# Attention and gated feed-forward on one core: casts of two batches at a projection, transposes in the gate/value parts, whole-tile stores, part of an exchange on Pool

## The chip, the cores and the metric

The kernel runs on one core of a Trainium2 chip. The metric is the device time of one execution in microseconds (us). Engines are named as the profile names them: PE (TensorE), DVE (VectorE), ACT (ScalarE), POOL (GpSimd) and SP (SyncE, which here only issues DMAs).

## What is computed

Attention without softmax, eight batches of twelve heads, 448 positions, 64 wide; then a gated feed-forward layer over all 3584 rows. Inputs and output are fp32; the kernel works in bf16 with fp32 accumulation.

```
scores = scale * q @ k.T                   # per batch and head, 448 x 448
attn   = max(scores, 0)**2 / S
x      = (attn @ v)  -> rows (batch, position), columns (head, d): 3584 x 768
out    = (max(x @ w_gate, 0) * (x @ w_val)) @ w_out      # 768 -> 1536 -> 768
```

## The kernel before

**Stages.** `first_batch` computes the attention of batch 0. Then for b = 1 to 7 the kernel runs the gate/value product of batch b-1 (`gv_units`, twelve units of 128 columns of d_ff, twelve steps of four matmuls each) with the attention of batch b woven in. `evenly` and `spread` do this: a list of events (score tiles, value passes, loads) is put between steps (unit, step) of the gate/value product. After the even b = 2, 4 and 6 and at the end, `out_pair` projects a pair of batches with w_out. Each engine's and queue's order is the order of the program (`pin`).

**Scores.** `tile_of` computes one pair of score tiles into one of two double PSUM banks; ACT takes the relu into `r_sb` (L230, four buffers), DVE squares it into `attn` (L231, two buffers of one quad each). There are 21 such tiles in a batch, in three quads (`qd`) of four heads. `values` multiplies a quad by v; ACT and DVE copy the result into `x[0]`, and `exchange` copies it with its halves of 64 partitions swapped into `x[1]` (L259). The gate/value product of the next stage reads both.

**Keys and queries.** `T_b` (`kqT`) holds them transposed, in two buffers used by even and odd batches. Batches 0 and 1 are transposed on PE (`transposes`). For the others, `load_qk(b)` casts keys and queries to bf16 in DRAM (two DMAs of POOL, `ks` and `qs`), and `dma_transposes(b, t)` transposes them into `kqT` by DMAs of SP: seven for the keys (L186), one for the queries (L179). `hold(b)` (L522) is a pair of tiny POOL copies out of `kqT`; since POOL works in order, the loads behind it are issued after the transposes have landed.

**When.** Before the change: casts of 2 after the first batch; its transposes in the last two units of b = 1, then a hold, w_out and casts of 3; transposes of 3 in the first projection; a hold, casts of 4 and v at b = 3; and so on, each cast behind a hold on the transposes before it. The transposes of 6 are issued in the second projection.

**The projection.** `out_pair` computes two blocks each way with seven block products instead of eight (A are the blocks of the hidden values `hT`, B of w_out). DVE forms sums of A blocks first (`sums`, L367). Sums of B blocks are formed once, by `weight_sums(0)` to `weight_sums(3)` (L324), in the last four units of b = 2: the third makes T2 and the fourth T4, both in `o_ring`. PE's products follow in the order A11·B11, A12·B21, A11·T2, S1·T1, A21·B12, A22·T4, A12·B22, each over four row tiles (three of 128 rows, one of 64). `keep` (ACT, L359) takes a product out of PSUM and `add` (DVE, L363) adds another. The results lie in the two `attn` buffers until `store_rows` (L377) has stored them; each tile's two halves of 64 rows go out by two DMAs, one of POOL and one of SP.

Of the kernel before, what the change touches and what calls it, by code (L numbers as in the profile page):

```python
# [16 lines left out]
def kernel(  # L17
# [22 lines left out]
    nc = tc.nc  # L40
# [28 lines left out]
    def pin(ins):  # L69
        return tc.keep_in_program_order(ins)  # L70
# [184 lines left out]

    def exchange(b, qd):
        a = slice(2 * qd, 2 * qd + 2)
        for (_, p), (_, other) in zip(HALVES, HALVES[::-1]):
            pin(nc.vector.tensor_copy(x_of[b][1][p, a, :], x_of[b][0][other, a, :]))  # L259

    def values(b, qd, ps):
        value_passes(b, qd, ps, 0, NC)
# [63 lines left out]
    def out_pair(b0, last, aside=None):  # L326
# [41 lines left out]

        def store_rows(t, r, c0, c1, engines):
            s0, n = tiles[t]  # L370
            for c in range(2):
                src = o_sb[2 * t + r][c * 64:c * 64 + 64, c0:c1, :]
# [4 lines left out]
                pin(engines[c].dma_start(out=rows[:, c0:c1, :], in_=src))  # L377

        pool, sync = ((e, e) for e in (nc.gpsimd, nc.sync))
        both, ends = (nc.gpsimd, nc.sync), (nc.sync, nc.scalar)  # L380
        for group in (((0, 1), (2, 3)) if last else ((0, 1, 2, 3),)):
            early = last and group[-1] == 3
            cols = slice(tiles[group[0]][0], sum(tiles[group[-1]]))
            sums(S1, A21, A22, ALU.add, cols)
            sums(A21, A11, A21, ALU.subtract, cols)
            for t in group:
                product(P, t, A11, B11, True)
                keep(t, 0, 0)
            sums(A11, S1, A11, ALU.subtract, cols)
# [36 lines left out]
    STRAIGHT = [(e, hp) for e in range(2) for hp in range(HP)]  # L426

# [121 lines left out]
    def turned(b, u0, u1):  # L549

        return [(u, 1, lambda t=t: dma_transposes(b, t)) for t, u in enumerate((u0, u1))]

    def held(b, u, *some):

        return [(u, 2, lambda: [hold(b)] + [load(c) for load, c in some if c < B])]

    new_x(0)
    units = gv_units(0)
# [3 lines left out]
    for b in range(1, B):  # L562
# [4 lines left out]
        events = evenly(units, {1: 2, 2: 4}.get(b, 0), last, events_of(b)) + [(last, 5, values_event(b, 2))]  # L567
# [46 lines left out]
```

## Time and profile before

| | |
|---|---|
| runs of the kernel | 418.74, 421.94, 415.93 us (median 418.74) |
| the profiled execution | 418.96 us, span 416.9 us, mean granted PE clock 0.997 |
| chain that ended last | PE 84%, DVE 6%, ACT 4%, issue 3%, DMA 3% |
| DMA | 44.26 MB in 155367 packets; POOL's queues 69.3% of 16 engines' span, SP's 20.4% |
| gate/value matmuls (L73, ps<-x,gv) | 4608 of 64x448, 253.2 us busy |
| relus of the scores (L230) | 168, mean 929 ns |
| squares (L231) | 168, mean 623 ns |
| exchange copies (L259) | 48, mean 444 ns |
| sums of A blocks (L367, 128x1344) | mean 850 ns, started some 770 ns apart |
| weight sums (L324) | 4, mean about 1350 ns |
| key and query transposes | 42 DMAs (median issue 1.25 us) and 6 (3.4 us) |

The span runs from the first to the last instruction; the execution's time is 2.06 us longer. The shares in the chain are of the work that ended last, followed back from the end. A line of a timeline holds the start, the time taken, the engine, the line of the kernel, the operation, its output and inputs and how many are merged; in brackets, the engine's idle time before it and what ended that. "SPq" and "ACTq" are DMA issues. In the view by stretches the columns are the stretch, its length, busy time (and instructions) of PE, PEld, DVE, ACT and POOL, PE's granted clock, DMA share and GB/s.

### The profile page before, as it was taken

How to read it: one execution, taken by the hardware profiler on the slowest of the kernel's cores; microseconds unless marked ns; L12 is line 12 of the kernel's file. 1: busy time of each engine (PE TensorE's matmuls, PEld its weight loads, DVE VectorE, ACT ScalarE, POOL GpSimd, SP SyncE). 2: the span in 40 equal slices, each digit the busy share in tenths (PEclk: the TensorE clock that was granted, in tenths of full speed). 3: DMA queues.
4: the chain of work that ended last, by engine and by line, in shares of the span. 5: the costliest groups of instructions: out<-in, count | busy, mean ns of one | idle time of the engine just before them, and what ended most of it. 6: DMA issues, size and time to landing. Idle time of an engine off the chain costs nothing.

```text
span 416.9 us, 16663 instructions
## 1 busy us (share of the span) xinstructions
PE 399.2 (96%) x7536; PEld 275.7 (66%) x7536; DVE 254.9 (61%) x449; ACT 235.4 (56%) x353; POOL 92.0 (22%) x123
## 2 busy tenths in 40 slices
PE   7899997999999998999999999999999999999994
PEld 4466775776776655776677677777777666666673
DVE  4986883589924775866743576676762567422551
ACT  4963991697335775767513877677623777322221
POOL 8834500630007303204304700020002100000040
PEclk9999999999999999999999999999999999999998
DMA  9999999799918995998998992460003600000053
GB/s 157 183 195 195 183 130 119 128 187 138 139 35 252 125 135 94 107 90 110 126 104 201 210 123 32 94 90 4 2 3 83 185 3 3 3 2 4 2 177 91
DMA packets 155367, 44.26 MB, mean 106 GB/s; under 512 B 131136, under 2 KB 153024, under 8 KB 155296
## 3 DMA queue, kind: packets, MB, share of 16 engines
q0 software_dynamic: 117376, 28.67, 69.3%
q1 hardware_dynamic: 37328, 14.03, 20.4%
q8 instruction: 59, 0.97, 1.0%
q10 hardware_dynamic: 592, 0.49, 0.5%
q14 instruction: 12, 0.10, 0.1%
HBM read 47.19 MB, written 19.27 MB: 159 GB/s over the span
## 4 chain that ended last, share of the span: by engine, by line
PE 84%; DVE 6%; ACT 4%; issue 3%; DMA 3%; SPq 0%; DVEq 0%; ACTq 0%
PE ps L73 82%; ACT r_sb L230 3%; DVE attn L231 3%; DMA out_dram<-attn 2%; DMA kr<-in_k_dram 1%; PE ps L206 1%; DVE kqT L207 1%; DVE hT L297 0%; DVE attn L363 0%; PE ps L215 0%; DVE qn L324 0%; DVE x L490 0%; SPq L377 0%; DVE x L259 0%; DVE kn L127 0%
## 5 line engine op out<-in xcount | busy, mean ns | idle before, releaser
L73 PE MATMUL ps<-x,gv 64*64 64x448 bf16 x4608 | 253.2, 349 | 4.2 <-issue 3.4
L73 PEld LDWEIGHTS <-gv 64*64 64x64 bf16 x4608 | 155.1, 107 | 72.8 <-issue 8.3
L230 ACT ACTIVATE r_sb<-ps 128x896 bf16<-128x896 f32 x168 | 149.1, 929 | 28.3 <-PE ps L73 24.2
L231 DVE TENSOR_TENSOR attn<-r_sb 128x896 bf16<-128x896 bf16 x168 | 102.8, 623 | 53.8 <-ACT r_sb L230 44.2
L297 DVE TENSOR_TENSOR hT<-ps,g_sb 128x448 bf16<-128x448 f32 x96 | 59.4, 620 | 34.1 <-ACT g_sb L296 33.6
L296 ACT ACTIVATE g_sb<-ps 128x448 bf16<-128x448 f32 x96 | 52.3, 546 | 48.2 <-PE ps L73 48.1
L73 PEld LDWEIGHTS <-hT 128*64 128x64 bf16 x1152 | 61.2, 110 | 22.6 <-issue 1.7
L73 PE MATMUL ps<-kqT 64*64 64x448 bf16 x672 | 69.2, 351 | 3.0 <-ACT r_sb L230 2.8
L359 ACT ACTIVATE attn<-ps 128x384 f32<-128x384 f32 x64 | 28.8, 450 | 61.1 <-PE ps L73 60.6
L73 PE MATMUL ps<-wo,hT 128*64 128x384 bf16 (+1 forms) x768 | 57.7, 306 | 0.0
L377 POOL DMA_DIRECT2D out_dram<-attn x32 | 17.6, 551 | 178.2 <-ACT attn L359 171.0
L363 DVE TENSOR_TENSOR attn<-ps,attn 128x384 f32<-128x384 f32 (+1 forms) x48 | 22.7, 503 | 45.0 <-ACT attn L359 27.7
L73 PE MATMUL ps<-attn,vn 64*64 64x448 bf16 x672 | 38.4, 350 | 2.6 <-issue 2.1
L73 PEld LDWEIGHTS <-kqT 64*64 64x64 bf16 x672 | 27.3, 106 | 16.5 <-issue 6.5
L73 PEld LDWEIGHTS <-vn 64*64 64x64 bf16 x672 | 23.6, 107 | 12.7 <-issue 4.4
L73 PE MATMUL ps<-o_ring,hT 128*64 128x384 bf16 (+1 forms) x384 | 29.6, 306 | 0.1
L263 ACT ACTIVATE x<-ps 128x448 bf16<-128x448 f32 x21 | 11.4, 543 | 30.3 <-PE ps L73 30.3
L115 POOL DMA_DIRECT2D vn<-in_v_dram x36 | 23.7, 677 | 13.3 <-DVE hT L297 5.0
L522 POOL COPY flag<-kqT 128x1 bf16<-128x1 bf16 x12 | 2.6, 231 | 107.1 <-DMA kqT<-ks 91.1
L259 DVE COPY x<-x 64x896 bf16<-64x896 bf16 x48 | 21.3, 444 | 2.7
L264 DVE CAST x<-ps 128x448 bf16<-128x448 f32 x21 | 13.1, 623 | 15.0 <-PE ps L73 14.9
L115 POOL DMA_DIRECT2D qs<-in_q_dram x6 | 14.8, 2462 | 4.3 <-issue 4.3
(43 smaller groups left out, 134.2 us busy)
## 6 DMA issues: line engine op xcount, KB each, us to landing
out_dram<-attn SPq DMA_DIRECT2D x22, 192.0 KB, 4.1
out_dram<-attn POOLq DMA_DIRECT2D x22, 192.0 KB, 4.4
ks<-in_k_dram POOLq DMA_DIRECT2D x6, 672.0 KB, 13.3
qs<-in_q_dram POOLq DMA_DIRECT2D x6, 672.0 KB, 17.1
vn<-in_v_dram POOLq DMA_DIRECT2D x14, 192.0 KB, 13.5
gv<-in_moe_w_gate_dram POOLq DMA_DIRECT2D x6, 384.0 KB, 11.7
gv<-in_moe_w_val_dram POOLq DMA_DIRECT2D x6, 384.0 KB, 11.4
wo<-in_moe_w_out_dram POOLq DMA_DIRECT2D x2, 1152.0 KB, 11.7
```

The costliest lines, as they stand in the source:

```text
L73: pin(nc.tensor.matmul(o, lhsT=l, rhs=r, start=start, stop=stop, skip_group_check=True))
L115: pin(nc.gpsimd.dma_start(out=o, in_=i))
L230: pin(nc.scalar.activation(r, src, AF.Relu))
L231: pin(nc.vector.tensor_tensor(dst, r, r, ALU.mult))
L259: pin(nc.vector.tensor_copy(x_of[b][1][p, a, :], x_of[b][0][other, a, :]))
L263: pin(nc.scalar.activation(x_of[b][0][:, 2 * qd, :], ps[:, 0, :S], AF.Copy))
L264: pin(nc.vector.tensor_copy(x_of[b][0][:, 2 * qd + 1, :], ps[:, 1, :S]))
L296: pin(nc.scalar.activation(g_sb, o[0], AF.Relu, scale=float(out_scale)))
L297: pin(nc.vector.tensor_tensor(hT[:, mf, col:col + S], o[1], g_sb, ALU.mult))
L359: pin(nc.scalar.activation(out_of(t, r, c), bank(P, t), AF.Copy))
L363: pin(nc.vector.tensor_tensor(o, bank(Q, t), o, ALU.add))
L377: pin(engines[c].dma_start(out=rows[:, c0:c1, :], in_=src))
```

## The change

- `exchange`: for b > 0 and the first two of three quads, POOL makes the two copies instead of DVE.
- Casts: `load_v(b + 2)`, `load_qk(b + 2)` and `load_qk(b + 3)` are issued just ahead of the projection after an even b. All holds but that on batch 2 are gone.
- Transposes: both parts of a batch are issued in one place (`turned`): unit 2 of a stage for b + 1, and for batch 3 the unit before the last of b = 2. For b = 1 the call stands in that branch (unit before the last) and also in the branch that all b but 2 pass through (unit 2).
- b = 1: its PE transposes and score tiles are spread from earlier steps.
- Weight sums: the first two in the last two units of b = 2, the other two in the first projection, behind the sums of A12.
- Stores: `out_pair(0)` keeps two DMAs for a tile; later pairs store a tile of 128 rows by one. Odd results (r = 1) go out by ACT, even ones by SP, none by POOL but in the last group.

```diff
     def exchange(b, qd):
         a = slice(2 * qd, 2 * qd + 2)
+        engine = nc.gpsimd if b > 0 and qd < NQ - 1 else nc.vector
         for (_, p), (_, other) in zip(HALVES, HALVES[::-1]):
-            pin(nc.vector.tensor_copy(x_of[b][1][p, a, :], x_of[b][0][other, a, :]))
+            pin(engine.tensor_copy(x_of[b][1][p, a, :], x_of[b][0][other, a, :]))
...
         def store_rows(t, r, c0, c1, engines):
             s0, n = tiles[t]
+            src = o_sb[2 * t + r]
+            if n == WHOLE and b0 >= NB:
+                row = (b0 + r) * S + s0
+                rows = out[row:row + n, :].rearrange("j (h m) -> j h m", h=2)
+                pin(engines[0].dma_start(out=rows[:, c0:c1, :], in_=src[:, c0:c1, :]))
+                return
             for c in range(2):
...
-        pool, sync = ((e, e) for e in (nc.gpsimd, nc.sync))
-        both, ends = (nc.gpsimd, nc.sync), (nc.sync, nc.scalar)
+        pool, sync, act = ((e, e) for e in (nc.gpsimd, nc.sync, nc.scalar))
+        ends = ((nc.sync, nc.scalar), (nc.scalar, nc.sync))
...
             sums(A12, A12, A11, ALU.subtract, cols)
-            if aside:
-                aside()
+            if first:
+                weight_sums(2)
+                weight_sums(3)
             for t in group:
                 product(P, t, A11, T2, False)
...
                     if not early:
-                        store_rows(t, 1, 0, 2, both)
+                        store_rows(t, 1, 0, 2, act)
                 if early:
                     for t in ts:
-                        store_rows(t, 1, 0, 1, ends)
+                        store_rows(t, 1, 0, 1, ends[0])
...
                     if early:
-                        store_rows(t, 0, 1, 2, ends)
+                        store_rows(t, 0, 1, 2, ends[1])
                     else:
-                        store_rows(t, 0, 0, 2, both)
+                        store_rows(t, 0, 0, 2, sync)
...
+    def turned(b):
+        for t in range(2):
+            dma_transposes(b, t)
+
+    def loads(*some):
+        return lambda: [load(b) for load, b in some if b < B]
...
         if b == 1:
-            events += [(1, 2 + 4 * qd, transposes_event(1, qd)) for qd in range(NQ)]
-            events += turned(2, last - 1, last) + [(last, 2, lambda: (hold(2), load_wo(), load_qk(3)))]
-        elif b == 2:
-            events += [(1, 1, lambda: load_v(3))]
-            events += [(8 + n, 3, lambda n=n: weight_sums(n)) for n in range(4)]
-        elif b == 3:
-            events += held(3, 0, (load_qk, 4), (load_v, 4)) + turned(4, 5, 6) + held(4, 7, (load_qk, 5))
-        elif even:
-            events += turned(b + 1, 1, 2) + held(b + 1, 3, (load_v, b + 1), (load_qk, b + 2)) if b + 1 < B else []
+            events = evenly(units, 1, last, [None] * 2 + events_of(b))[2:]
+            events += [(n, 8 - 4 * (n == 1), transposes_event(1, n)) for n in range(2)] + [(2, 0, transposes_event(1, 2))]
+            events += [(last - 1, 1, lambda: turned(2)), (last, 2, lambda: (hold(2), load_wo(), load_qk(3)))]
+        else:
+            events = evenly(units, {2: 4}.get(b, 0), last, events_of(b))
+        events.append((last, 5, values_event(b, 2)))
+        if b == 2:
+            events += [(1, 1, lambda: load_v(3)), (last - 1, 1, lambda: turned(3))]
+            events += [(last - 1 + n, 3, lambda n=n: weight_sums(n)) for n in range(2)]
         elif b + 1 < B:
-            events += held(b + 1, 0, (load_v, b + 1), (load_qk, b + 2))
+            events += [(0, 2, loads((load_v, b + 1 if even else B)))] + [(2, 1, lambda: turned(b + 1))]
         spread(units, events)
         if even:
-            t = b + 1 if b == 2 else b + 2
-            out_pair(b - 2, False, (lambda: [dma_transposes(t, n) for n in range(2)]) if t < B else None)
+            loads((load_v, b + 2), (load_qk, b + 2), (load_qk, b + 3))()
+            out_pair(b - 2, False)
```

More of the change, by code (lines that the diff above doesn't have):

```diff
@@ L324, in weight_sums, with out_pair @@
         pin(nc.vector.tensor_tensor(o, a, b, op))
-    def out_pair(b0, last, aside=None):
+    def out_pair(b0, last):
+        first = b0 == 0
         hT = hT_of[b0]
@@ L370, in store_rows @@
             s0, n = tiles[t]
+            src = o_sb[2 * t + r]
[4 more added lines that the diff above has]
+                return
             for c in range(2):
-                src = o_sb[2 * t + r][c * 64:c * 64 + 64, c0:c1, :]
                 rows = segment_rows(b0, r * NC + s0 // 64 + (c if n == WHOLE else 0))
@@ L376, in store_rows @@
                     rows = rows[:, :, c * (OH // 2):(c + 1) * (OH // 2)]
-                pin(engines[c].dma_start(out=rows[:, c0:c1, :], in_=src))
-        pool, sync = ((e, e) for e in (nc.gpsimd, nc.sync))
-        both, ends = (nc.gpsimd, nc.sync), (nc.sync, nc.scalar)
+                pin(engines[c].dma_start(out=rows[:, c0:c1, :], in_=src[c * 64:c * 64 + 64, c0:c1, :]))
+        pool, sync, act = ((e, e) for e in (nc.gpsimd, nc.sync, nc.scalar))
+        ends = ((nc.sync, nc.scalar), (nc.scalar, nc.sync))
         for group in (((0, 1), (2, 3)) if last else ((0, 1, 2, 3),)):
@@ L547, in evenly @@
         return [(u, min(n, len(units[u]) - 4), e) for (u, n), e in zip(places, events)]
[L549 to L555, printed above, removed]
+    def turned(b):
[3 more added lines that the diff above has]
+        return lambda: [load(b) for load, b in some if b < B]
     new_x(0)
@@ L566 @@
         even = b % 2 == 0
-        events = evenly(units, {1: 2, 2: 4}.get(b, 0), last, events_of(b)) + [(last, 5, values_event(b, 2))]
         if b == 1:
-            events += [(1, 2 + 4 * qd, transposes_event(1, qd)) for qd in range(NQ)]
-            events += turned(2, last - 1, last) + [(last, 2, lambda: (hold(2), load_wo(), load_qk(3)))]
-        elif b == 2:
-            events += [(1, 1, lambda: load_v(3))]
-            events += [(8 + n, 3, lambda n=n: weight_sums(n)) for n in range(4)]
-        elif b == 3:
-            events += held(3, 0, (load_qk, 4), (load_v, 4)) + turned(4, 5, 6) + held(4, 7, (load_qk, 5))
-        elif even:
-            events += turned(b + 1, 1, 2) + held(b + 1, 3, (load_v, b + 1), (load_qk, b + 2)) if b + 1 < B else []
+            events = evenly(units, 1, last, [None] * 2 + events_of(b))[2:]
[7 more added lines that the diff above has]
+            events += [(last - 1 + n, 3, lambda n=n: weight_sums(n)) for n in range(2)]
         elif b + 1 < B:
-            events += held(b + 1, 0, (load_v, b + 1), (load_qk, b + 2))
+            events += [(0, 2, loads((load_v, b + 1 if even else B)))] + [(2, 1, lambda: turned(b + 1))]
         spread(units, events)
         if even:
-            t = b + 1 if b == 2 else b + 2
-            out_pair(b - 2, False, (lambda: [dma_transposes(t, n) for n in range(2)]) if t < B else None)
+            loads((load_v, b + 2), (load_qk, b + 2), (load_qk, b + 3))()
+            out_pair(b - 2, False)
     spread(gv_units(B - 1), [])
```

## The prediction

> **What bounds the kernel now.** I read the busy shares first, then busy time by stretches of time, then the queues' timelines around the changed steps.
>
> ```profile
> PE 399.2 (96%) x7536; PEld 275.7 (66%) x7536; DVE 254.9 (61%) x449; ACT 235.4 (56%) x353; POOL 92.0 (22%) x123
> ```
> ```profile
> 60.00:70.00 10.00, 8.05 (x168) 5.77 (x164) 5.27 (x10) 4.03 (x7) 0.00 (x0) 1.00 1.76 123
> 80.00:90.00 10.00, 9.71 (x208) 7.18 (x203) 8.32 (x15) 8.99 (x14) 5.97 (x5) 1.00 1.14 204
> 280.00:290.00 10.00, 10.00 (x216) 7.60 (x212) 6.82 (x12) 7.57 (x11) 0.00 (x0) 1.00 0.02 4
> ```
>
> PE is full (216 matmuls in 10 us) wherever nothing disturbs it. What can be won is small: the stretch 60 to 70 lacks some 48 matmuls (2.2 us), 80 to 105 lacks 1 to 2 us with DVE and ACT at eight to nine tenths. What can be lost is any wait of PE, one for one.
>
> ```profile
> 56.59 12.66 SPq L186 DMA_TRANSPOSE kqT<-ks  x7
> 69.35 4.17 SPq L179 DMA_TRANSPOSE kqT<-qs  x1
> ```
> ```profile
> 257.85 9.65 SPq L186 DMA_TRANSPOSE kqT<-ks  x6
> 267.60 2.79 SPq L179 DMA_TRANSPOSE kqT<-qs  x1
> ```
> ```profile
> 77.10 0.19 POOL L522 COPY flag<-kqT 128x1 bf16<-128x1 bf16 x1 [3.45 <-DMA kqT<-qs]
> 272.74 0.19 POOL L522 COPY flag<-kqT 128x1 bf16<-128x1 bf16 x1 [3.65 <-DMA kqT<-qs]
> ```
> ```profile
> 65.88 0.57 PE L73 MATMUL ps<-attn,vn 64*64 64x448 bf16 x8 [1.90 <-issue]
> 72.90 5.11 PE L73 MATMUL ps<-x,gv 64*64 64x448 bf16 x104 [0.77 <-issue]
> 77.81 0.39 PE L73 MATMUL ps<-kqT 64*64 64x448 bf16 x4
> ```
>
> A set of transposes is eight DMAs on SP's queue, 56.59 to 73.52 for batch 2. Its flag on POOL runs at 77.10, when the last has landed, and PE reads the result at 77.81. There is no slack. The two "issue" waits of PE lie 128 matmuls apart while transposes run. The page counts 59 DMAs of kind "instruction" with 0.97 MB, so 16 KB each, room for 128 matmuls with their weight loads; I read these waits as instructions that arrive late.
>
> **The change, part by part.** The durations are of one execution: span 416.9, its time 418.96, 0.22 above the median of 418.74.
>
> *1. Batch 2 is transposed twice.* For b = 1 the new code adds turned(2) in its own branch, and again in the branch for every b that isn't 2. SP's order in the changed program has the eight DMAs of batch 2 twice, and PE's first scores of batch 2, as well as the hold on POOL, wait for the second set. The first set depends on casts, not on PE, so it keeps its times, and SP is free for the second at 73.52. The nearest row is batch 7, alone on the DMA engines: 257.85 to 272.74 is 14.9 us for seven of the eight, and 1.2 for the eighth makes 16.1. That gives 89.6; the first set's last DMA still runs until 77.1, so I take 90.5. PE starts at 90.7 instead of 77.81: **+12.9**. Ends: +10 (issue alone, seven at 1.25 and one at 3.4, and 2 to land) and +16.4 (20.5 us, as the first set took beside casts). All that b = 1 gains by spreading its scores and transposes, and its two waits for instructions, ends in this wait: 0. Behind the hold on POOL stand the loads of wo, the casts of batch 3 and v of batch 3, 13 us later. Before, wo lands at 92.8 and batch 3's transposes are issued by 114.3; the changed order uses them from about 103 and 130, and both uses move by the same 13: 0, and 1 us for each us if that cover went.
>
> *2. PE's clock after 13 us of idling.*
>
> ```profile
> 1.10:4.50 3.40, 3.34 (x18) 1.61 (x20) 1.87 (x7) 1.86 (x2) 3.15 (x6) 1.00 0.69 166
> 414.20:416.90 2.70, 0.00 (x0) 0.00 (x0) 0.00 (x0) 0.00 (x0) 0.00 (x0) 0.50 0.23 56
> ```
> At the start, 18 blank matmuls, nine pairs, take 3.34 us, 0.37 a pair, where a pair of 448 columns takes 0.19 later; at the end the granted clock is 0.50, some 3 us after the last matmul. So a restart costs 3.4 us at half speed: **+1.7** (0 to 1.9).
>
> *3. Batch 2's stage.* Two of its four weight sums (1.35 us each) leave for the projection, two move to its end, and four copies of 0.39 us go to Pool. I take half of the 2 us missing in 80 to 105: **-1.0** (0 to -1.8).
>
> *4. The weight sums in the first projection.*
>
> ```profile
> 105.84 7.03 PE L73 MATMUL ps<-wo,hT 128*64 128x384 bf16 x96
> ...
> 112.56 1.74 DVE L363 TENSOR_TENSOR attn<-ps,attn 128x384 f32<-128x384 f32 x4
> 112.70 3.59 PE L73 MATMUL ps<-o_ring,hT 128*64 128x384 bf16 x48
> ...
> 114.22 1.61 DVE L367 TENSOR_TENSOR hT<-hT 128x1344 bf16<-128x1344 bf16 x2
> ```
> At 112.70 PE goes straight on to o_ring. In the changed order DVE makes o_ring only behind the four additions and the two sums of A12. DVE comes there about 0.85 us earlier, since no weight sum stands before its last x; then additions to 113.4, sums to 115.0, weight sum 2 to 116.4. PE waits 112.7 to 116.4: **+3.7** (3.0 to 5.4, the upper end with another restart of the clock).
>
> *5. Stores on ACT and SP, beside casts.*
>
> ```profile
> 124.66 3.46 SPq L377 DMA_DIRECT2D out_dram<-attn  x4
> ```
> ```profile
> 128.56 5.76 SPq L377 DMA_DIRECT2D out_dram<-attn  x4
> ```
> ```profile
> 232.24 1.16 DVE L231 TENSOR_TENSOR attn<-r_sb 128x896 bf16<-128x896 bf16 x2 [3.81 <-DMA out_dram<-attn]
> 233.99 0.38 PE L73 MATMUL ps<-x,gv 64*64 64x448 bf16 x2 [0.36 <-DVE hT L297]
> ```
> After each of three projections ACT issues all stores of the odd rows: eight DMAs in the first, five (three of twice the size) later. SP's first four of such a group took about 0.5 us each, the last four 1.1 to 1.8, the queue being full. At 0.5 ACT is done before the next stage wants its first relu: 0. At 1.1 to 1.8 it is busy until 3 to 5 us into the stage, and with two score banks PE loses 1.5 to 3. The casts of two batches now run beside the stores of pairs one and two, so these land later too, and DVE's first attn waits for them as at 232.24. I take 1.0 each, **+3.0** (0 to 9). On SP the transposes of batches 4 and 6 stand behind these stores; they begin some 4 us into a stage of 34 and take 17, and PE wants them at its end: 0. POOL, without stores, issues the casts earlier: 0 but for that company.
>
> *6. Late instructions.* Before: 1.67 in batch 4's transposes, 0.95 in batch 5's beside a cast, none for 6 (in a projection), 0.24 for 7. After: batch 4's still run beside casts (1.7), 5's and 7's alone (0.24 each), 6's leave the projection for the gate/value part with a cast beside them (0.95). **+0.3** (-2.6 to +3). The Trainium skill, page "Runtime: NRT & Kernel Launch", section "Instruction fetch mechanics", says that crossing a 16 KiB block is mostly hidden. By that rule this term would be 0 and the sum 438.6; the trace, with waits of 1.90 and 1.45 us at such steps, disagrees.
>
> *7. Pool's 28 copies.* No row has Pool copy 64x896. From Pool's select of 128 columns (332 ns) and its copy of one (187 ns), about 1.2 us each. Their readers come a stage later, so the length itself is covered; **+0.5** for DVE meeting them (0 to 3).
>
> *8. The end.*
>
> ```profile
> 408.39 5.89 SPq L377 DMA_DIRECT2D out_dram<-attn  x8
> ```
> After PE's end SP still works off eight issues, 0.7 us apart, past DVE's last addition at 411.35. With whole tiles and swapped queues it has six: **-1.2** (0 to -1.9).
>
> Sum: 12.9 + 1.7 - 1.0 + 3.7 + 3.0 + 0.3 + 0.5 - 1.2 = +19.9, so 438.9 against 418.96, or **438.7** against the median.
>
> **The rivals.**
> *Lighter:* ACT issues at 0.5 us, the second set lands at 89, the clock costs little: +12 to +14, 431 to 433. For it, SP's first four issues; against it, the casts beside.
> *ACT's queue fills* (issues of 1.1 to 1.8 in every pair, stores late by the casts): term 5 becomes 9 to 11, 446. For it the 5.76 us for four; against it, ACT's four at the end took about 0.5 each.
> *Pool's copies shut DVE out.* One row shows such a thing: two copies took 2.57 us instead of 0.79 while POOL issued a cast.
> ```profile
> 166.82 2.57 DVE L259 COPY x<-x 64x896 bf16<-64x896 bf16 x2
> ```
> If each of Pool's four copies in batch 2's stage holds DVE for 1.2 us, term 3 is +3.2 instead of -1.0: 443. Elsewhere DVE, 68% busy in 280 to 290, absorbs it. The Trainium skill, page "SBUF — State Buffer", section "SBUF: two separate sides", has the rule: Pool and DVE share one port pair, locked for a whole instruction. The row at 166.82 agrees; no row shows Pool copies doing it.
> *Not slower:* the second set costs PE nothing, because its rewriting lands before PE comes. That takes terms 1 and 2 away and gives b = 1's spreading 0.8: 423.3, within 2%. It decides if the second set lands by about 81, within 7.5 us of SP's becoming free. Against it, no set in the trace takes under 14.
>
> **How the numbers follow.** Forecast 0.62 (433 to 444 by its terms' middles), ACT's queue 0.17, Pool's lock 0.09, lighter 0.08, not slower 0.04. The time is the forecast's, 438.7. The range 430 to 447.5 takes in lighter, the lock and most of the full queue, and leaves out under 2 in 10. A measurement here tells about 2% from no change (410.4 to 427.1). Slower by over 2%: all but the last case, 0.95; within 2%: 0.04; faster: 0.01, for which every term would have to fail.
>
> **What would show it.** Two sets for batch 2 on SP, the second ending near 88 and landing near 90; PE idle some 13 us before its first kqT of that stage, with half clock behind it. PE idle 3 to 4 us before its first o_ring, with DVE's two L325 sums right before. ACT's L377 and L384 at 0.5 (term 5 too high) or over 1 us (too low). DVE's attn rows of 0.6 us grown beside Pool's L260. It is wrong at its root if the second set is missing or short.

## The result, and the profile after

| | before | after |
|---|---|---|
| median (range, runs) | 419.5 (415.93 to 421.94, 4) | 451.34 (449.84 to 453.44, 4) |
| ratio, with 95% interval | | 1.077 (1.067 to 1.087) |
| the profiled execution: time, span | 418.96, 416.9 | 449.84, 448.0 |
| its mean granted PE clock | 0.997 | 0.964 |

The change makes the kernel 7.7% slower. The direction was forecast with 0.95, but the time lies above the range of 430 to 447.5. Ratios and their intervals, here and below, leave out executions in a slow state, such as one of 595.78 us among the four of a later run. To see where the 31.1 us of span went, compare when PE starts the same piece of work in both profiled executions:

| PE starts | before | after | shift | added since the row above |
|---|---|---|---|---|
| first scores of batch 2 | 77.81 | 88.79 | +10.98 | 10.98 |
| first projection | 105.84 | 117.97 | +12.13 | 1.15 |
| its third product (o_ring) | 112.70 | 129.29 | +16.59 | 4.46 |
| stage of batch 3 | 129.90 | 148.05 | +18.15 | 1.56 |
| second projection | 203.90 | 231.52 | +27.62 | 9.47 |
| third projection | 299.93 | 332.67 | +32.74 | 5.12 |
| PE's last matmul | 410.71 | 443.44 | +32.73 | 0 |
| end of the span | 416.9 | 448.0 | +31.1 | -1.6 |

So there are four places: the transposes of batch 2, the weight sums, and the beginnings of the stages behind the first and second projections. From the third projection on, everything runs as before.

The timeline of SP in the profile after, around batch 2; the numbers are start, time taken, queue, line, operation and how many:

```profile
57.05 12.24 SPq L186 DMA_TRANSPOSE kqT<-ks  x7
69.40 4.69 SPq L179 DMA_TRANSPOSE kqT<-qs  x1
74.14 9.26 SPq L186 DMA_TRANSPOSE kqT<-ks  x7
83.45 3.24 SPq L179 DMA_TRANSPOSE kqT<-qs  x1
```

The second set is there, as forecast, directly behind the first. These are PE's longest waits in the profile after (what, for whom: total us, times, longest). Before, PE waited 3.1 us in all for ACT's r_sb and 0.4 for DVE's hT, and the other three lines have no match there:

```profile
PE ps L73 <- DMA kqT<-qs: 9.6, 1, 9.6
PE ps L73 <- ACT r_sb L230: 7.1, 9, 3.0
PE ps L73 <- ACT attn L361: 5.7, 1, 5.7
PE ps L73 <- DVE o_ring L325: 4.3, 1, 4.3
...
PE ps L73 <- DVE hT L298: 3.2, 1, 3.2
```

The first line is the second set, the fourth the weight sums. The third and the last lie behind the projections, as PE's timeline shows; so do 4.3 us of the second:

```profile
155.83 0.58 PE L73 MATMUL ps<-kqT 64*64 64x448 bf16 x2 [5.70 <-ACT attn L361]
266.04 0.58 PE L73 MATMUL ps<-x,gv 64*64 64x448 bf16 x2 [3.22 <-DVE hT L298]
```

This is the beginning of batch 3's stage after the change, on ACT, DVE, SP and POOL in turn (their timelines):

```profile
142.82 2.18 ACTq L384 DMA_DIRECT2D out_dram<-attn  x2
...
149.45 5.96 ACTq L384 DMA_DIRECT2D out_dram<-attn  x2
155.45 0.33 ACT L361 ACTIVATE attn<-ps 128x192 f32<-128x192 f32 x1 [6.03 <-issue]
156.09 4.47 ACTq L384 DMA_DIRECT2D out_dram<-attn  x2
160.66 1.73 ACT L230 ACTIVATE r_sb<-ps 128x896 bf16<-128x896 f32 x2 [4.88 <-issue]
```
```profile
162.15 1.16 DVE L231 TENSOR_TENSOR attn<-r_sb 128x896 bf16<-128x896 bf16 x2 [13.62 <-DMA out_dram<-attn]
```
```profile
144.84 18.62 SPq L384 DMA_DIRECT2D out_dram<-attn  x8
```
```profile
119.73 2.43 POOL L115 DMA_DIRECT2D ks<-in_k_dram  x1
122.15 2.43 POOL L115 DMA_DIRECT2D qs<-in_q_dram  x1
141.70 2.39 POOL L115 DMA_DIRECT2D ks<-in_k_dram  x1 [17.13 <-issue]
146.67 2.40 POOL L115 DMA_DIRECT2D qs<-in_q_dram  x1 [2.58 <-issue]
```

ACT needs 10.4 us for its last four issues, and SP 18.6 for its eight (before, SP took 5.8 for the last four of its eight). Before the change, DVE wrote its first square of this stage 3 us after PE had begun the stage, and waited for no store:

```profile
133.04 1.16 DVE L231 TENSOR_TENSOR attn<-r_sb 128x896 bf16<-128x896 bf16 x2 [2.67 <-ACT r_sb L230]
```

Now it waits until a store has landed, 14 us after PE's start. POOL's casts of batch 5 run beside all of this. The view of DMA issues in that stretch (KB each, median us from issue to landing), before and after:

```profile
out_dram<-attn SPq DMA_DIRECT2D x6, 192.0 KB, 4.4
out_dram<-attn POOLq DMA_DIRECT2D x6, 192.0 KB, 4.4
```
```profile
out_dram<-attn ACTq DMA_DIRECT2D x6, 192.0 KB, 11.4
out_dram<-attn SPq DMA_DIRECT2D x6, 192.0 KB, 10.9
```

A store takes 11 us instead of 4.4. Either ACT's queue or the company of the casts can be the reason; the profile alone does not tell which.

### The profile page after: what moved, and what is told of

It reads as the page before. It is cut to its first block, busy times and chain, and to the rows that moved or that the text cites. A ratio compares the mean times of both kernels' runs of the same rounds, so it can differ in the third digit from the quotient of the medians.

```text
span 448.0 us, 16588 instructions
## 1 busy us (share of the span) xinstructions
PE 407.4 (91%) x7536; PEld 283.0 (63%) x7536; DVE 250.4 (56%) x421; ACT 235.7 (53%) x353; POOL 100.6 (22%) x112
## 4 chain that ended last, share of the span: by engine, by line
PE 79%; DMA 7%; DVE 5%; SPq 4%; issue 2%; ACT 2%; ACTq 1%; DVEq 0%
PE ps L73 77%; DMA out_dram<-attn 5%; SPq L186 2%; DVE attn L231 2%; DMA kqT<-qs 1%; SPq L179 1%; DMA kr<-in_k_dram 1%; ACT r_sb L230 1%; ACTq L384 1%; PE ps L206 1%; DVE attn L365 1%; DVE kqT L207 1%; DVE hT L369 0%; ACT attn L361 0%; DVE o_ring L325 0%
## 5 line engine op out<-in xcount | busy, mean ns | idle before, releaser
L73 PE MATMUL ps<-x,gv 64*64 64x448 bf16 x4608 | 259.7, 355 | 5.7 <-DVE hT L298 3.2
L73 PEld LDWEIGHTS <-gv 64*64 64x64 bf16 x4608 | 162.2, 109 | 73.1 <-issue 7.9
L231 DVE TENSOR_TENSOR attn<-r_sb 128x896 bf16<-128x896 bf16 x168 | 111.2, 672 | 85.3 <-ACT r_sb L230 60.0
L73 PE MATMUL ps<-kqT 64*64 64x448 bf16 x672 | 72.9, 359 | 22.9 <-DMA kqT<-qs 9.6
L260 POOL COPY x<-x 64x896 bf16<-64x896 bf16 x28 | 26.9, 960 | 175.3 <-DVE x L265 174.4
L73 PEld LDWEIGHTS <-kqT 64*64 64x64 bf16 x672 | 29.4, 108 | 37.6 <-issue 27.6
L365 DVE TENSOR_TENSOR attn<-ps,attn 128x384 f32<-128x384 f32 (+1 forms) x48 | 22.8, 505 | 48.3 <-ACT attn L361 31.1
L73 PE MATMUL ps<-o_ring,hT 128*64 128x384 bf16 (+1 forms) x384 | 31.1, 316 | 4.4 <-DVE o_ring L325 4.3
L264 ACT ACTIVATE x<-ps 128x448 bf16<-128x448 f32 x21 | 11.4, 543 | 29.5 <-PE ps L73 29.5
L265 DVE CAST x<-ps 128x448 bf16<-128x448 f32 x21 | 13.1, 623 | 15.3 <-PE ps L73 15.3
L115 POOL DMA_DIRECT2D ks<-in_k_dram x6 | 14.5, 2422 | 24.2 <-issue 23.9
L115 POOL DMA_DIRECT2D qs<-in_q_dram x6 | 14.5, 2417 | 9.8 <-issue 9.8
L73 PE MATMUL ps<-qn,kn 128*64 128x384 bf16 (+1 forms) x192 | 14.5, 306 | 0.0
## 6 DMA issues: line engine op xcount, KB each, us to landing
gv<-in_moe_w_val_dram POOLq DMA_DIRECT2D x6, 384.0 KB, 10.9
```

Of the source, the lines that this page charges most:

```text
L73: pin(nc.tensor.matmul(o, lhsT=l, rhs=r, start=start, stop=stop, skip_group_check=True))
L115: pin(nc.gpsimd.dma_start(out=o, in_=i))
L231: pin(nc.vector.tensor_tensor(dst, r, r, ALU.mult))
L260: pin(engine.tensor_copy(x_of[b][1][p, a, :], x_of[b][0][other, a, :]))
L264: pin(nc.scalar.activation(x_of[b][0][:, 2 * qd, :], ps[:, 0, :S], AF.Copy))
L265: pin(nc.vector.tensor_copy(x_of[b][0][:, 2 * qd + 1, :], ps[:, 1, :S]))
```

## The experiments

Two theories were set against each other. *Crowding*: the casts, small packets on the same DMA engines (in that stretch 17017 of them for 1.64 MB on their queue), delay the stores, so that the issuing queues block and the attn buffers come free late. (No run separates the size of the packets from the bytes moved.) *ACT's queue*: the issuing itself, on an engine that has relus to do, is the cost. Ratios are against runs of the kernel before on the same chip.

**One set of transposes.**

```diff
-        elif b + 1 < B:
+        elif b > 1 and b + 1 < B:
             events += [(0, 2, loads((load_v, b + 1 if even else B)))] + [(2, 1, lambda: turned(b + 1))]
```

> The changed kernel with one set of transposes for batch 2 instead of two. If the second set is what PE waited for (11.0 us up to its first scores of batch 2, and 1.2 us more by the clock behind that wait), the time falls by 10 to 12.5 us, to 439 to 441. Rival: the first set, crowded by the casts, would by itself have landed late or the wait only moves to the next thing (w_out, the casts of batch 3, which would now start about 13 us earlier): then it falls by less than 8. The set should end near 74 and land near 77, PE's first scores of batch 2 stand near 78 to 79, and the loss around the stores of pairs one and two (14.6 us) stays.

438.22 us, ratio 1.045 (1.036 to 1.054): 13.1 us less than the change by the medians. PE's first scores of batch 2 are at 78.10 and the first projection starts at 106.06, where the kernel before has 77.81 and 105.84. The medians thus give the second set 13.1 us, a little over the upper end of the expectation, with some 4 us of noise; in the profiles the first projection starts 11.9 us earlier (106.06 against 117.97). The loss behind the projections stays: the shift grows from 7.5 us at the stage of batch 3 to 18.4 at the second projection and 23.1 at the third.

**The casts of batches 5 and 7 held behind the stores**, which ACT and SP issue as in the changed kernel. A small POOL copy out of the first square of the next stage's second quad waits for the landed stores; the casts follow it in POOL's order.

```diff
-            loads((load_v, b + 2), (load_qk, b + 2), (load_qk, b + 3))()
+            loads((load_v, b + 2), (load_qk, b + 2))()
...
+            if n == NC and b in (3, 5):
+                e[-1] = lambda s=e[-1]: (s(), behind(attn_of(b, 1)), load_qk(b + 2))
```

> The changed kernel, but the casts of batches 5 and 7 are issued only when the eighth score tile of the next stage has been squared, which is behind the landing of all stores of the pair; ACT issues the same stores as in the changed kernel. Theory of crowding (the casts share the DMA engines with the stores, so these land 10 to 13 us after their issue, ACT's issue blocks, and attn's buffers come free late): the 14.6 us of the stages of batches 3 and 5 fall to 1 to 4, the time falls by 10.5 to 14 us, to 437 to 441; stores land 3 to 6 us after issue. Rival, ACT's queue by itself (a DMA's issue holds up the relus behind it whatever else runs): it falls by 0 to 3 us, to 448 to 451, and ACT's issues stay at 4 to 6 us each two.

435.43, ratio 1.040 (1.032 to 1.047): 15.9 us less than the change. The stages of batches 3 and 4 now add 1.4 us, those of 5 and 6 nothing (-0.2). The DMA issues of this kernel at its first projection, then DVE's first square:

```profile
out_dram<-attn ACTq DMA_DIRECT2D x6, 192.0 KB, 4.7
out_dram<-attn SPq DMA_DIRECT2D x6, 192.0 KB, 5.1
```
```profile
154.04 1.16 DVE L231 TENSOR_TENSOR attn<-r_sb 128x896 bf16<-128x896 bf16 x2 [5.07 <-DMA out_dram<-attn]
```

The same queues issue the same stores, these land in 5 us instead of 11, and of the 14.6 us behind the projections 1.2 are left (15.9 us by the medians, 13.4 by the stages). That is crowding.

**The odd rows by SP, casts as in the change.**

```diff
-                        store_rows(t, 1, 0, 2, act)
+                        store_rows(t, 1, 0, 2, act if last else sync)
```

> The changed kernel, but the odd rows of pairs one to three are stored by SP, not ACT; casts beside them stay. ACT's queue by itself: ACT's relus are free at once, the time falls by 6 to 9 us (PE's waits for ACT's attn and r_sb of 5.7, 3.0 and 1.4 us go, with the half clock behind them), to 442 to 445. Theory of crowding: the stores still land late and DVE's first attn of the stage still waits for them, now all on one queue: it falls by 0 to 4 us, or rises up to 3, since SP issues 16 stores one behind the other in pair one.

450.33, ratio 1.074: 1.0 us less than the change, inside the spread of the two (449.04 to 450.64, and 449.84 to 453.44). In the profile the same stages add 14.7 us, where the change adds 14.6. ACT is free of issues, and PE waits no more for ACT's attn; it waits for DVE instead, which waits for the stores (PE's waits, then DVE's timeline):

```profile
PE ps L73 <- DVE hT L298: 15.4, 2, 12.0
```
```profile
163.81 1.16 DVE L231 TENSOR_TENSOR attn<-r_sb 128x896 bf16<-128x896 bf16 x2 [15.46 <-DMA out_dram<-attn]
```

ACT's blocked relus were a symptom; taking them away only shows the next wait. The Trainium skill, page "DMA: Bandwidth & Descriptors", section "Issuing engines are not separate DMA queues", says that DMAs issued by different engines run on the same DMA engines, so that spreading them saves only issue time. This pair of runs agrees: taking the issues off ACT gave at most about 1 us, inside the noise, and taking the company away gave 15.9.

**All weight sums back in batch 2's stage** (the two calls in the projection removed, `weight_sums(n)` for four n in the last four units).

> The changed kernel with all four sums of w_out's blocks back in the last four units of batch 2's stage, none in the projection. PE's wait of 4.45 us for the third sum goes, and with it 1.5 us of half clock; DVE gets 1 us more work in the stage: the time falls by 4 to 6 us, to 445 to 447.5. Rival: the wait is only the next thing's (the sums of the A blocks, which stood before it on DVE, or w_out's landing, 13 us later than before the change, so that the sums in the stage now stop DVE's squares): it falls by less than 2 us.

444.46, ratio 1.062: 6.9 us less. PE goes from the first product to o_ring without a stop (120.37 to 127.23, 6.86 us, as in the kernel before). The rival falls. The gain is above the expectation by a microsecond, well inside its noise of some 4 us. The profiled execution (448.12, the slowest of four) shows something on the other side: with all four weight sums in it, batch 2's stage adds 4.0 us up to the projection where the change adds 1.15, and some 1.7 of these 2.9 are half clock, which lasted 13.7 us behind the second set instead of 10.2.

**All three mended, and with DVE making the exchange again.** The first joins the three edits above; the second also has `engine = nc.vector`.

> The changed kernel with the three mended together: one set of transposes for batch 2, the casts of batches 5 and 7 behind the stores, all sums of w_out's blocks in batch 2's stage. If the second set, the crowded stores and PE's wait for o_ring are the whole loss, the time is back at the kernel before, less what the end gives (1.6 us) and plus the 1 to 1.5 us that ACT's issues still cost the stage of batch 3: 416.5 to 420.5, ratio 0.993 to 1.003. Rival: something that all three runs shared and that stays (Pool's copies, the spread of batch 1, transposes beside other work in every stage, the clock) costs 3 us or more: over 422.

> As the one with three mended, but DVE makes all exchange copies, as before the change. If Pool's copies hold DVE up so that PE feels it, this is 1 to 3 us faster than the one with Pool's copies; if they only lengthen squares that are covered (16 to 18 of them took 0.74 to 1.36 us instead of 0.62), the two agree within 0.7 us; if the relief of DVE was worth something, this one is 0.5 to 1.5 us slower.

421.55 (ratio 1.009, 1.006 to 1.012) and 424.12 (1.013, 1.009 to 1.017). Both miss: some 4 us are still lost, nearly all in the beginning of batch 3's stage (shift 0.6 at its start, 4.5 at the second projection, with Pool's copies). With one set of transposes the first projection starts 11.5 us earlier than in the change, and the casts of batch 4, which are not held, now run into its stores: the last is issued at 110.1 and lands at 140.6, the stores go out from 125 to 139. So the stores were crowded again, this time by another batch's casts. With DVE's copies another wait came up: SP did not issue the transpose of batch 3's queries until 130.86, and PE waited 6.7 us for it. So the pair does not price Pool's copies by its totals. Batch 2's stage does: from its first scores to the projection it takes 29.96 us with Pool's copies, 28.51 with DVE's, 28.03 in the kernel before. DVE's squares there (line, shapes and count, then busy us and mean ns), first with Pool's copies, then with DVE's own:

```profile
L231 DVE TENSOR_TENSOR attn<-r_sb 128x896 bf16<-128x896 bf16 x21 | 15.8, 761 | 2.7 <-ACT r_sb L230 2.4
```
```profile
L231 DVE TENSOR_TENSOR attn<-r_sb 128x896 bf16<-128x896 bf16 x21 | 12.8, 623 | 2.5 <-ACT r_sb L230 2.1
```

The relief of 1.6 us (four copies of 0.39) costs DVE 3.0 us in longer squares.

**Only Pool's copies, in the kernel before** (the first two lines of the change's diff).

> The kernel before, but Pool makes the 28 exchange copies as in the changed kernel. If a Pool copy keeps DVE from its two-input squares while it lasts, DVE's 21 squares of batch 2's stage grow from 0.62 to about 0.76 us (3 us in all, against 1.6 us of copies saved), and PE loses 1 to 2 us in that stage, where DVE also has the weight sums; elsewhere nothing: ratio 1.002 to 1.005. If DVE's relief is worth what I forecast in term 3, it is 0.5 to 1 us faster.

420.6, ratio 1.009 (1.005 to 1.013), by which it is 2 to 5 us slower, more than I had expected. In batch 2's stage the 21 squares again have a mean of 761 ns and PE loses 2.2 us. This kernel's POOL and DVE timelines show why:

```profile
93.76 2.72 POOL L260 COPY x<-x 64x896 bf16<-64x896 bf16 x2
```
```profile
94.33 2.63 DVE L231 TENSOR_TENSOR attn<-r_sb 128x896 bf16<-128x896 bf16 x2
```

Two squares of 0.62 us take 1.3 each while Pool copies. The Trainium skill's rule that I cited in my third rival ("SBUF — State Buffer", section "SBUF: two separate sides") names this very pair, a DVE operation with two SBUF inputs against a GpSimd operation that reads SBUF; the rows agree. The other 2 us are an effect of queue order that I had not expected: Pool's copies stand behind its holds, and at the start of batch 4's stage PE waits 2.6 us for `POOL x L260` and has half clock for 3.4.

**The end alone, in the kernel before** (whole tiles and the changed queues for the last pair only).

> The kernel before with nothing but the changed stores of the last pair (whole tiles, odd rows of the first group by ACT, swapped queues at the end). If the end's gain stands by itself, 1.2 to 1.9 us faster than the kernel before: 417.3 to 418.2, ratio 0.9955 to 0.997. Rival: what the changed kernel gained at its end came from elsewhere (its clock, its queues being empty): 0 to 0.5 us.

417.07, ratio 0.9959 (0.9923 to 0.9995), by which it is 1.7 us faster, with an interval from 0.2 to 3.2. The change's last edit holds what term 8 said.

**The mended kernel with the odd rows by Pool.**

> As the one with three mended and DVE's copies, but the odd rows of pairs one to three are stored by Pool, whose queue is empty there since the casts wait. If ACT's issues still hold up the relus of batch 3's stage, this is 1 to 1.5 us faster than its neighbour and 1.5 to 3 us faster than the kernel before; if the queue that issues plays no part once the casts are away, the two agree within 0.7 us.

424.23, ratio 1.015: no better than its neighbour. Pool's queue was not empty, as I had written, since the casts of batch 4 stand in it. Its stores land 14.5 us after issue in the first pair, SP's beside them 6.9.

**Casts added where there were none: at the third pair.** Four casts into spare rows, then eight; the edit shown is that of the eight, and four have `range(2)`.

```diff
+            if b == 6:
+                for n in range(4):
+                    for src in (k, q):
+                        spare = dram.tile([S, H, D], BF16, name=f"spare{n}{src is q}")
+                        dma_in(spare.rearrange("s h d -> h s d"), src[n])
             out_pair(b - 2, False)
```

> The changed kernel, in which the third pair's stores, with no casts beside them, cost nothing; added are four casts of keys and queries into spare rows ahead of that pair's projection (extra work, read by nothing). Theory of crowding: the same stores by the same queues now land 8 to 13 us after their issue, and the stage of batch 7 loses 3.5 to 7 us, as that of batch 5 does (5.1): 455 to 458.5. Rival, by which casts only look guilty (the loss of pairs one and two comes from their place: the transposes behind them, v's loads, Pool's copies): 0 to 1 us, 451 to 452.5.

448.84, ratio 1.074. No loss, but no test either: Pool was free at 320.17, the four casts had all landed by 349.0, and the ten stores were issued from 346.9 to 353.3.

> The changed kernel with eight casts into spare rows ahead of the third pair's projection instead of four (extra work, read by nothing): with four, the last had landed at 349.0, when only two of ten stores had been issued, so the two hardly met. A cast took 5 to 6.6 us, so eight run to about 372, past all stores. Theory of crowding: the third pair's stores land 8 to 13 us after their issue instead of 2 to 4, and the stage of batch 7 loses 3.5 to 7 us (0 before), 452 to 458. Rival, casts only look guilty: stores as before, 0 to 1 us, 448 to 452.

453.99, ratio 1.087. Between the third projection and the fourth the shift against the kernel before now grows by 6.58 us (after: 0.00). The same stores in the changed kernel, then with eight casts beside them:

```profile
out_dram<-attn ACTq DMA_DIRECT2D x3, 384.0 KB, 2.9
out_dram<-attn SPq DMA_DIRECT2D x3, 384.0 KB, 4.1
```
```profile
out_dram<-attn ACTq DMA_DIRECT2D x3, 384.0 KB, 8.4
out_dram<-attn SPq DMA_DIRECT2D x3, 384.0 KB, 8.5
```

The total says less than the stage, since this run had lost less than the change ahead of the third projection. Casts can be added to make the loss and held to take it away, with the stores untouched.

**v held too.** As the three mended, but v of batches 4 and 6 is loaded behind the stores.

> As the one with three mended, but v of batches 4 and 6 is loaded behind the stores too, so that only the casts of batch 4 stand ahead of the first projection. There the last cast, of batch 4's queries, landed at 140.6, beside the stores of 125 to 139, and PE lost 4 us at 132 to 144. Theory of crowding: without v's four DMAs that cast lands 3 to 6 us earlier, the stores land earlier, and the loss shrinks to 0.5 to 2.5 us: 1.5 to 4 us faster than the one with three mended, 417.5 to 420. Rival, by which that loss is not the cast's: less than 1 us faster, or slower since v comes late.

423.13, ratio 1.014 (1.008 to 1.019). The place came out as the theory says: the last cast of batch 4 landed at 132.2, and from the start of batch 3's stage to the second projection only 1.5 us were lost instead of 3.9. The total did not, as 3.3 us came up in the stages of batches 5 and 6, where v, a cast and transposes now meet. PE's timeline there:

```profile
256.21 1.30 PE L73 MATMUL ps<-attn,vn 64*64 64x448 bf16 x23
260.70 0.54 PE L73 MATMUL ps<-attn,vn 64*64 64x448 bf16 x5 [3.19 <-issue]
```

**The changed stores alone, in the kernel before.**

> The kernel before with all of the changed stores (odd rows by ACT, even rows by SP, whole tiles after the first pair) and its casts where they were, behind the holds. Theory of crowding: ACT's issues by themselves cost at most the 1.4 us that the stage of batch 3 kept when the casts were held, and the end gives 1.6: ratio 0.995 to 1.001. ACT's queue by itself: 4 us or more slower, ratio over 1.01.

433.61, ratio 1.041 (1.036 to 1.046). By the number this is the case of ACT's queue, and crowding, which gave 418.5 at most, missed by 15 us. The trace shows a third thing, though: in the first pair ACT's issues take 0.5 to 0.7 us each, and it is SP that waits. SP's timeline:

```profile
104.82 3.92 SPq L186 DMA_TRANSPOSE kqT<-ks  x3
127.34 3.46 SPq L179 DMA_TRANSPOSE kqT<-qs  x1
```

The transposes of batch 3 stand in the projection in this kernel. The DMAs of SP and ACT take eight completion semaphores in turn, and a DMA waits until its semaphore's last user has landed: in the traces of all these runs a semaphore was used again 1547 times, never before that. In the order that the program was given, that was ACT's first store (issued 124.57, landed 127.28). SP went on at 127.34, PE waited 3.8 us for the result (the profile gives that wait the name of the store, which shares the semaphore), and at the second projection SP's stores in their turn stood behind transposes until 242.75 (DVE idle 12.4 us for a store). There is no crowd here: the casts went out behind the stores, at 134.49 and 247.88, and the first pair's stores landed in 3.0 to 3.7 us (medians). The 5.9 and 10.0 us that the two stages lose are the price of the shared turn. The same wait is what came up with DVE's copies above: there the first store landed at 130.80, and SP went on at 130.86. In the changed kernel no transpose stands there, but the stores themselves wait in this turn: each of the six store issues from 155.79 to 161.76 starts 0.02 to 0.10 us behind the landing of its semaphore's last user. So stores that land late are also what blocks the two issuing queues.

**The same with the odd rows by SP.**

> The kernel before with the changed stores, but the odd rows of pairs one to three by SP instead of ACT. With them on ACT it lost 15.5 us: SP did not issue the transpose of batch 3's queries until 127.34, right behind the landing of ACT's first store at 127.28, since the DMAs of SP and ACT share eight semaphores in turn, and PE waited for what came late. If that sharing is the cause, SP alone issues in one order, the transposes go out ahead of the stores, and the time is that of the kernel before, less 1.6 at the end and plus 0 to 4 for 16 stores on one queue: 416.5 to 422. Rival, the transposes beside the stores are late whoever issues: 428 or more.

428.28, ratio 1.027 (1.019 to 1.034). With all stores on SP the transpose is issued at 109.65, about as before (109.80), so the loss by sharing is gone. Yet only 5.3 us come back, and 10.9 are lost behind the two projections. The total is the rival's, the reason is not, for the transposes are no longer late; PE waits 11.7 us for DVE's hT, and DVE for stores. POOL's timeline shows what had changed, first in the kernel before, then in this one:

```profile
130.38 1.14 POOL L377 DMA_DIRECT2D out_dram<-attn  x2 [0.20 <-DVE attn L363]
...
131.75 2.47 POOL L115 DMA_DIRECT2D ks<-in_k_dram  x1
134.21 2.42 POOL L115 DMA_DIRECT2D qs<-in_q_dram  x1
```
```profile
118.08 2.43 POOL L115 DMA_DIRECT2D ks<-in_k_dram  x1 [0.17 <-issue]
120.50 2.43 POOL L115 DMA_DIRECT2D qs<-in_q_dram  x1
```

In the kernel before, Pool's share of the stores stood ahead of the next casts in Pool's own order. It held them back until the stores were out. Without stores, and with the transposes in time for Pool's hold on them, Pool runs on and casts beside the stores, 13.7 us earlier: one loss has taken the place of the other.

**The same, with only the casts held.** In the stages of batches 3 and 5 a copy out of the first square stands ahead of the casts that follow (batches 4 and 7) and of the loads of v.

```diff
+            events += [(0, 2, lambda: behind(attn_of(3, 0)))]
             events += held(3, 0, (load_qk, 4), (load_v, 4)) + turned(4, 5, 6) + held(4, 7, (load_qk, 5))
...
+            events += [(0, 2, lambda b=b: behind(attn_of(b, 0)))]
             events += held(b + 1, 0, (load_v, b + 1), (load_qk, b + 2))
```

> The kernel before with its stores on SP as in the last run, but Pool issues the casts of batches 4 and 7 (and the loads of v beside them) only behind the first squared score tile of the next stage, so behind the landing of the first half of the pair's stores. In the last run Pool, freed from the stores, issued these casts from 118.1 and 222.9 on, before the stores, and these landed 7 to 8 us after issue instead of 3 to 6; 10.9 us went in the two stages. Theory of crowding (Pool's stores were, in the kernel before, what held the casts back): these 10.9 us fall to 0 to 4, 416.5 to 421.5. Rival (SP's single queue of 16 stores is the cost): it stays at 425 to 429.

414.66, ratio 0.9936 (0.9906 to 0.9965): 13.6 us faster than its twin, faster than the kernel before by 2.6 us, and the fastest of all. Its profiled execution took 419.88, the longest of its ten, so only the order and the landing times are read from it: the stores of the first pair, in its twin and in it,

```profile
out_dram<-attn SPq DMA_DIRECT2D x12, 192.0 KB, 7.4
```
```profile
out_dram<-attn SPq DMA_DIRECT2D x12, 192.0 KB, 3.0
```

and the casts are issued from 136.40 on. SP's single queue of 16 stores costs nothing that shows once it is alone.

## Why the prediction was wrong

| term | forecast | measured |
|---|---|---|
| 1, second set | +12.9 | +11.0 (13.1 with the clock behind it, by removing it) |
| 2 and 3, clock and DVE's relief in batch 2's stage | +0.7 | +1.15 |
| 4, weight sums in the projection | +3.7 | +6.0: 4.46 of waiting and 1.56 of half clock |
| 5, 6 and 7, behind the projections | +3.8 | +14.6 |
| 8, the end | -1.2 | -1.6 |
| sum | +19.9 | +31.1 |

**Term 1 was right**, place and mechanism; it was 1.9 us too long, because I built it up from batch 7's transposes and let the first set's last DMA push it. All eight of the second set landed 14.6 us after SP came free; batch 7's 14.9 was for seven of its eight.

**Term 4 was right in its wait** (4.46 us within 3.0 to 5.4), and wrong to leave the clock to the upper end. The wait is 0.76 above the 3.7 because I gave DVE a head start of 0.85 us, "since no weight sum stands before its last x". One still does, in DVE's timeline after, and the additions begin 6.7 us behind PE's start of the projection, as before:

```profile
116.73 1.35 DVE L325 TENSOR_TENSOR wo<-wo,wo 128x2304 bf16<-128x2304 bf16 x1
118.00 0.62 DVE L265 CAST x<-ps 128x448 bf16<-128x448 f32 x1
...
124.68 1.75 DVE L365 TENSOR_TENSOR attn<-ps,attn 128x384 f32<-128x384 f32 x4
```

Windows of the profile after (PE's granted clock is the third number from the end):

```profile
74.00:88.70 14.70, 5.11 (x104) 3.71 (x104) 1.88 (x3) 1.63 (x3) 0.18 (x1) 0.75 0.63 126
129.30:132.50 3.20, 3.20 (x22) 1.84 (x24) 1.33 (x1) 0.49 (x1) 0.00 (x0) 0.51 1.64 144
148.00:168.00 20.00, 11.33 (x152) 6.59 (x152) 4.11 (x9) 6.17 (x9) 1.07 (x1) 0.66 1.70 191
```

A wait of 4.3 us is enough: the clock was at 0.51 for the 3.2 us behind it.

**Term 5 failed**, and it carries 10.8 of the 11.2 us by which the span's growth exceeds the forecast. I wrote: "these land later too, and DVE's first attn waits for them as at 232.24. I take 1.0 each, +3.0 (0 to 9)." The mechanism was named; its size was wrong, and no working stands behind the 1.0. The row beside it, a wait of DVE of 3.81 us in the kernel before, cost PE 0.36 and was for a store that landed 6.4 us after its issue (225.75 to 232.11). I had no row with casts beside the stores. With them the stores landed in 11 us, and the stages behind two projections took 9.5 and 5.1 us longer, term 6's gain included; the one behind the third, without casts, took no longer. The held casts (-15.9 us by the medians, -13.4 by the stages), the added casts (+6.6) and the last twin pair (13.6 us) show that it is the casts' company that makes the size. I also priced ACT's issues as a cost of their own, from 0.5 or 1.1 to 1.8 us each; with the odd rows on SP the stages lose as much as before, so these issues cost nothing that shows of themselves. My rival *ACT's queue fills* came nearest in its number (446) and had late stores in its condition; the full queue, from which it took its name and its price, was an effect of them.

I also set at nothing "POOL, without stores, issues the casts earlier: 0 but for that company." In the kernel before, Pool's stores do keep the casts off the other stores; the twin pair puts a price on that, 13.6 us by the medians and 10.9 by the stages of the run without it. In the changed kernel the casts are placed ahead of the projection by the edit itself, so there they run beside the stores whoever issues them (with the odd rows by Pool, in the mended kernel, these landed 14.5 us after issue, behind casts).

**Term 6** came out at its lower end: PE's waits for "issue" behind batch 1, 2.8 us before, are gone after the change, so that the 14.6 is a net figure. **Term 3 and 7** belong together, and their rival *Pool's copies shut DVE out* was right in kind: 21 squares of 761 ns instead of 623. In the changed kernel PE felt little of it, probably since two weight sums had left the stage (with all four back in the change, the stage took 2.9 us more, 1.7 of them half clock); where all four stood there and one set of transposes ran, Pool's copies cost 1.5 to 2.2 us. The 1.15 itself varies: two runs with the same code up to the first projection show 2.9 and 3.1. **Term 8** was right, alone too (1.7 us).

What stays open: how much of the 14.6 is the blocked issue and how much the late buffers. Both go when the casts go, and the six issues named above were themselves blocked by late landings; no run separates the two further. Nor does any run tell whether it is the casts' many small packets or their bytes that delay the stores.

## What to carry to other kernels

When an instruction leaves a queue, list what stood behind it: in the kernel before, the stores on Pool's queue also kept the casts away from the other stores, an order that no line of the code spells out. With only the stores moved (odd rows by SP), losing it cost 11 to 14 us, far more than any issue time saved. Price a transfer's landing by a row with the same company on the DMA engines, not by its issue or by a row where it was nearly alone. When the blame falls on a queue, change the queue and the company in separate runs; here the one gave about 1 us, inside the noise, and the other 15.9.

## What the runs showed of the hardware

- Stores of 192 KB at the first projection landed 3.0 to 5.2 us after issue (medians) where the casts' queue moved few packets beside them (290 to 5400), and 6.6 to 11.4 us where it moved 11500 to 20800. Behind casts in their own queue they took 14.5 us (odd rows by Pool).
- A DMA issued by SP or ACT waits for the landing of the last DMA with the same completion semaphore; eight are taken in turn by both. A transpose on SP went out at 127.34, 0.06 us behind the landing of ACT's store of 124.57, and PE waited 3.8 us for it (the changed stores in the kernel before).
- PE's half clock comes in pieces of 3.4 us: away from both ends of these traces it lasted 3.4, 6.8, 10.2 or 13.7 us. Waits of 4.3 us (after, at o_ring) and even of 2.0 and 0.6 close together (Pool's copies in the kernel before, at 171) brought a piece, one of 3.2 us (v held, at 260.70) brought none.
- Of Pool and DVE, whoever begins first makes the other wait: a weight sum begun inside a Pool copy (106.72, sums in the stage) took 2.08 us instead of 1.35; one begun 0.2 us ahead of two copies (111.39, the same run) took its 1.34, and the copies 3.20 instead of the 1.9 that two take undisturbed.
- PE waited 3.19 us at 260.70 with v held, when casts, v and transposes shared the DMA engines. The trace names no releaser, but the wait ends 1.5 us behind the landing of a DMA of 16384 bytes of the kind "instruction" (259.19), as does the one of 1.90 us at 65.88 in the kernel before (64.27; 1.6 us): late instructions, as the prediction read such waits.
